# Adding the mirrored rows by accumulating DMAs instead of by VectorE, in a Fourier-mixing and leaky-ReLU kernel

## The chip, the cores and the metric

The kernel runs on one core of one Trainium2 chip. The metric is the device time of one execution in microseconds (us), the median of three runs. The profile is that of one execution, taken by the hardware profiler; its engines are PE (TensorE matmul), PEld (TensorE weight load), DVE (VectorE), ACT (ScalarE), POOL (GpSimd) and SP (SyncE, which here only issues DMAs). A name such as L287 is a line of the kernel before.

## The reference

```python
batch, seq, dim = (8, 3008, 256)          # x: float32
n_tokens, d_model, d_ff = (24064, 256, 2048)

def _attn_ref(x):
    X = np.fft.fft(x, axis=1)
    X = np.fft.fft(X, axis=2)
    return X.real.astype(np.float32)

def _moe_ref(x, w_in, w_out):
    h = x @ w_in
    g = np.maximum(0.01 * h, h)
    return (g @ w_out).astype(np.float32)

# x -> _attn_ref -> reshape to (B*S, D) -> _moe_ref
```

The real part of a two-dimensional Fourier transform of each batch is taken, and every row of it goes through an up projection, a leaky ReLU and a down projection.

## The kernel before

The cosine and sine transforms along the sequence use symmetries: row s and row S-s of x, and the half-turn rows around S/2, are added or subtracted before any matmul, so that a batch needs only a small part of the products. The host lays x out so that a row and its mirror lie at the same place of two planes: index 0 of the third axis of the tile is the row, index 1 its mirror.

```python
def x_tile():
    return xp.tile([LOADED, 2, 2, NT, D], F32, tag="x", bufs=1, name="xt")   # LOADED=128, NT=8, D=256

def load_x(b):
    t = x_tile()
    for h in range(2):
        for odd in range(2):
            load_rows(t, b, h, odd)
    return t

def load_rows(t, b, h, odd):                 # L280: 1024 KB each, four for a batch
    nc.sync.dma_start(t[:, h, :, odd * NI[0] : NI[0] + odd * NI[1]], x[b, h, odd])

def add_mirrors(t, h, rows):                 # L287
    a, z = t[:, h, 0, rows], t[:, h, 1, rows]
    nc.vector.tensor_tensor(a, a, z, op=ALU.add)

def fold_columns(t, h, part, rows):          # L294, L296
    a, z = t[:, h, 0, rows], t[:, h, 1, rows]
    if part == 0:
        nc.vector.tensor_tensor(z[:, :, 0:P], a[:, :, 0:P], a[:, :, P:D], op=ALU.add)
    else:
        nc.vector.tensor_tensor(z[:, :, P + 1 : D], a[:, :, 1:P], a[:, :, P + 1 : D], op=ALU.subtract)

def fold_halves(t, part, c, rows, to=None):  # L303: reads both z planes, writes t[:, i, 0]
    ...

def fold_x(b, at):                           # at = 0 .. 7
    t, rows = xs[b], slice(0, NT)
    h, i = divmod(at, 2)
    if h < 2 and i == 0:
        add_mirrors(t, h, rows)
    elif h < 2:
        for part in range(2):
            fold_columns(t, h, part, rows)
    else:
        fold_halves(t, i, 3 - h, rows)
    if at == 7:
        zs[b] = xs.pop(b)
```

The work is cut into 16 units (8 batches, each with the odd and the even frequencies), 3 blocks of about 251 columns in a unit and 8 steps `f` in a block: 384 steps. A step raises a block with two of the hidden layer's sixteen 128-row groups (`up`) and lowers the one of three steps earlier (`down`). The first two blocks use a plain form; the others use seven products instead of eight, for which GpSimd makes four sums `s1` to `s4`.

```python
def up(j, f):            # raised: 4 matmuls into two banks (L734), then activate:
    ...
    nc.vector.scalar_tensor_tensor(cos[:, hs], ...)          # L743, two of them
    nc.vector.tensor_tensor(g[:, 0], cos, sin bank, add)     # L747 (shortened)
    nc.vector.tensor_tensor(g[:, 1], cos, sin bank, subtract)# L748 (shortened)
    nc.scalar.activation(g, g, ACT.Lrelu)                    # L749
    nc.gpsimd.tensor_tensor(s1 ... s4)                       # L756 to L759

def down(j, f):
    if f == 0:
        banks = [sum_ps() for _ in range(4)]     # all four banks of the tag "sum"
    ...                                          # 7 matmuls, L801, in the order 0 1 5 6 4 2 3
    if f < NH - 1:
        return
    nc.scalar.copy(q1, p1)                       # L810
    for to, x, y in ((c11, q1, p2), (u2, q1, p6), (u3, u2, p7), (v, u2, p5),
                     (c22, u3, p5), (c12, v, p3), (c21, u3, p4)):
        nc.vector.tensor_tensor(to, x, y, op=ALU.add)        # L812
    put(o, n, first)

lag = 3
folds = {(0, 1): (0,), (0, 3): (1,), (0, 4): (2,), (0, 5): (3,), (0, 6): (4, 5), (0, 7): (6,), (1, 0): (7,)}

def step(at):
    j, f = steps[at]
    up(j, f)
    n, part = divmod(j, 3)
    b, c = units[n]
    if 0 < n < len(units) - 1:
        ...
        if n % 2 == 1 and (part, f) in folds:
            for i in folds[part, f]:
                fold_x(b + 1, i)
        if part > 0 and f == 3:
            fold_rows(units[n + 1], part - 1)    # ScalarE turns L323, L324; VectorE L326, L327 and others
        if part > 0 and f == 5:
            dft(units[n + 1], part - 1)          # matmuls from xt, L572
    if n % 2 == 0 and part == 2 and f == 6 and b + 1 < B:
        xs[b + 1] = load_x(b + 1)
    if at - lag >= done:
        down(*steps[at - lag])
```

The table `folds` says at which step the source asks for a part of the fold. In the main loop the tile framework orders each engine's instructions when the kernel is built, by its own estimate of when they are ready, and the engines run that fixed order on the chip: the fold of a batch comes some steps earlier than the table asks. The first batch is loaded and folded by other code ahead of the loop, which the change leaves as it is.

`turn`, which `fold_rows` uses, lets ScalarE write two scaled copies into the scratch that was the plane of the mirrored rows:

```python
nc.scalar.activation(tmp[0], y, ACT.Copy, scale=sin)   # L323
nc.scalar.activation(tmp[1], y, ACT.Copy, scale=cos)   # L324
```

Of the kernel before, what the change touches and what calls it, by code (L numbers as in the profile page):

```python
# [60 lines left out]
ALU = mybir.AluOpType  # L61
# [3 lines left out]
P = 128  # L65
H, Q = S // 2, S // 4

NI = [4, 4]
# [170 lines left out]
def tile_fnet_leaky_relu(  # L239
# [12 lines left out]
    nc = tc.nc  # L252
# [13 lines left out]
    def x_tile():  # L266
        return xp.tile([LOADED, 2, 2, NT, D], F32, tag="x", bufs=1, name="xt")
# [2 lines left out]
        return ps.tile([P, 512], F32, tag="sum", bufs=4, name="sum_ps")  # L270

    def load_x(b):
        t = x_tile()
        for h in range(2):
            for odd in range(2):
                load_rows(t, b, h, odd)
        return t

    def load_rows(t, b, h, odd):
        nc.sync.dma_start(t[:, h, :, odd * NI[0] : NI[0] + odd * NI[1]], x[b, h, odd])  # L280
# [3 lines left out]
# [5 lines that stand above are left out]
    def fold_columns(t, h, part, rows):  # L289
# [8 lines that stand above are left out]
    def fold_halves(t, part, c, rows, to=None):  # L298

        i, cols = (c + part) % 2, slice(part * P, (part + 1) * P)  # L300
        z = t[:, :, 1, rows, cols]
        to = t[:, i, 0, rows, cols] if to is None else to[:, rows]
        nc.vector.tensor_tensor(to, z[:, 0], z[:, 1], op=(ALU.add, ALU.subtract)[i])  # L303

    def fold_x(b, at):

        t, rows = xs[b], slice(0, NT)
        h, i = divmod(at, 2)
        if h < 2 and i == 0:
            add_mirrors(t, h, rows)  # L310
        elif h < 2:
            for part in range(2):
                fold_columns(t, h, part, rows)
        else:
            fold_halves(t, i, 3 - h, rows)
        if at == 7:
            zs[b] = xs.pop(b)
# [501 lines left out]
    def step(at):  # L819
        if at < len(steps):  # L820
# [4 lines that stand above are left out]
            if n == 0 and f in (2, 5):  # L825
                dft(units[1], f // 5)
            if 0 < n < len(units) - 1:
                if part == 0 and f == 4:
                    spread(units[n + 1])
# [4 lines that stand above are left out]
                    fold_rows(units[n + 1], part - 1)  # L834
                if part > 0 and f == 5:
                    dft(units[n + 1], part - 1)
# [4 lines that stand above are left out]
# [10 lines left out]
    with tc.manual_schedule(engines={mybir.EngineType.DVE, mybir.EngineType.PE, mybir.EngineType.SP}):  # L851
        with tc.manual_schedule(engines={mybir.EngineType.Pool, mybir.EngineType.Activation}):
# [8 lines left out]
            t = x_tile()  # L861
# [67 lines left out]
            odd = [direct.odd_rows(P, *first) for direct in (cosine, sine)]  # L929
# [6 lines left out]
            odd = [direct.odd_rows(P, *others) for direct in (cosine, sine)]  # L936
# [105 lines left out]
```

## Time and profile before

The median is 1901.75 us, of three runs from 1901.07 to 1901.96. The profiled execution has a span of 1900.0 us and a granted TensorE clock of 0.999.

| what | busy us, share of the span | instructions |
|---|---|---|
| PE | 1894.0, 100% | 9124 |
| PEld | 1684.1, 89% | 9124 |
| DVE | 1286.1, 68% | 2565 |
| POOL | 1113.6, 59% | 1509 |
| ACT | 502.0, 26% | 681 |
| DMA, all queues | 78.13 MB, mean 41 GB/s | 33052 packets |
| of it the loads of x (L280) | 32 of 1024 KB, median 9.1 us from issue to landing | |

How to read it: the busy share of an engine is an average over all stages. An engine that is idle costs nothing as long as the one that sets the end does not wait for it. PE's matmuls are pipelined and their ends are modelled, so a single matmul has a mean of 374 ns here while the next starts about 210 ns after it. In the timeline each row is the start in us, the duration in us, the engine, the line and operation, the tiles written and read, the shape and how many were merged into the row; square brackets tell the idle time ahead of it and what ended that.

### The profile page before, as it was taken

The numbers are of one execution on the slowest core, as the hardware profiler recorded it, in microseconds if no ns is written. First come the engines' busy times: TensorE is split into PE (matmuls) and PEld (weight loads), VectorE is DVE, ScalarE is ACT, GpSimd is POOL, SyncE is SP. The second block draws the span as 40 slices with busy tenths as digits, with TensorE's granted clock in tenths as the row PEclk, the third lists the DMA queues.
The fourth block names the chain that finished last, engine by engine and source line by source line (L and its number), as shares of the span: only waits on it lengthen the run. The fifth ranks groups of instructions, "written<-read, shape, count | busy, mean of one in ns | idle before, by whom it ended". The sixth has DMA issues, their size and how long they took to land.

```text
span 1900.0 us, 25328 instructions
## 1 busy us (share of the span) xinstructions
PE 1894.0 (100%) x9124; PEld 1684.1 (89%) x9124; DVE 1286.1 (68%) x2565; ACT 502.0 (26%) x681; POOL 1113.6 (59%) x1509
## 2 busy tenths in 40 slices
PE   9999999999999999999999999999999999999999
PEld 7888888988889888898888988889888888888988
DVE  8879755696656965569555796558865688556554
ACT  3532222222222322223222232222322223222221
POOL 2137655576555765558555575557655566555554
PEclk9999999999999999999999999999999999999999
DMA  7212000020002000020000200002000030000000
GB/s 274 78 31 108 12 20 22 30 90 12 31 12 85 34 20 22 12 108 11 23 20 12 108 23 12 19 12 108 23 12 20 12 119 12 20 12 23 12 11 23
DMA packets 33052, 78.13 MB, mean 41 GB/s; under 512 B 5264, under 2 KB 18960, under 8 KB 32928
## 3 DMA queue, kind: packets, MB, share of 16 engines
q1 hardware_dynamic: 32352, 76.52, 11.0%
q8 instruction: 73, 1.20, 0.3%
q14 instruction: 51, 0.42, 0.1%
q10 hardware_dynamic: 576, 0.00, 0.0%
HBM read 51.79 MB, written 24.71 MB: 40 GB/s over the span
## 4 chain that ended last, share of the span: by engine, by line
PE 98%; DMA 1%; DVE 0%; SPq 0%; issue 0%; DVEq 0%
PE sum_ps L801 58%; PE cos_ps L734 17%; PE sin_ps L734 17%; PE sum_ps L781 3%; PE dft_ps L572 3%; PE wf_ps L516 1%; DMA direct<-in_direct_tab_dram 1%; DMA xt<-in_x_dram 0%; PE dft_ps L399 0%; PE sum_ps L707 0%; DVE e L812 0%; DVE xt L287 0%; SPq L280 0%; SPq L449 0%; DVE differences L303 0%; DVE xt L294 0%
## 5 line engine op out<-in xcount | busy, mean ns | idle before, releaser
L749 ACT ACTIVATE g<-g 128x1004 f32<-128x1004 f32 (+1 forms) x384 | 399.2, 1040 | 1110.5 <-DVE g L748 1044.1
L743 DVE SCALAR_TENSOR_TENSOR cos<-nb,wn,cos_ps 128x251 f32<-128x251 f32 (+1 forms) x768 | 330.2, 470 | 517.5 <-PE cos_ps L734 514.2
L756 POOL TENSOR_TENSOR s<-g 128x251 f32<-128x251 f32 (+1 forms) x368 | 275.3, 748 | 655.9 <-ACT g L749 655.9
L801 PE MATMUL sum_ps<-s,wt 128*128 128x251 f32 (+1 forms) x2208 | 528.5, 374 | 0.0
L801 PEld LDWEIGHTS sum_ps<-s,wt 128*128 128x128 f32 x2208 | 415.0, 188 | 55.1 <-POOL s L757 2.2
L734 PE MATMUL cos_ps<-mix,wf 128*128 128x251 f32 (+1 forms) x1536 | 388.1, 375 | 0.0
L734 PE MATMUL sin_ps<-mix,wf 128*128 128x251 f32 (+1 forms) x1536 | 387.6, 374 | 0.0
L801 PE MATMUL sum_ps<-g,wo 128*128 128x251 f32 (+1 forms) x1472 | 373.0, 375 | 0.0
L757 POOL TENSOR_TENSOR s<-s,g 128x251 f32<-128x251 f32 (+1 forms) x368 | 325.4, 884 | 0.0
L734 PEld LDWEIGHTS cos_ps<-mix,wf 128*128 128x128 f32 x1536 | 291.1, 190 | 34.8 <-issue 1.1
L734 PEld LDWEIGHTS sin_ps<-mix,wf 128*128 128x128 f32 x1536 | 290.4, 189 | 34.6
L801 PEld LDWEIGHTS sum_ps<-g,wo 128*128 128x128 f32 x1472 | 276.9, 190 | 31.9
L759 POOL TENSOR_TENSOR s<-g,s 128x251 f32<-128x251 f32 (+1 forms) x368 | 275.2, 748 | 28.9
L747 DVE TENSOR_TENSOR g<-cos,sin_ps 128x502 f32<-128x502 f32 (+1 forms) x384 | 259.3, 675 | 42.6 <-DVE cos L743 5.7
L748 DVE TENSOR_TENSOR g<-cos,sin_ps 128x502 f32<-128x502 f32 (+1 forms) x384 | 256.9, 669 | 0.0
L758 POOL TENSOR_TENSOR s<-g 128x251 f32<-128x251 f32 (+1 forms) x368 | 249.1, 677 | 0.0
L801 PE MATMUL sum_ps<-g,wt 128*128 128x251 f32 (+1 forms) x736 | 215.8, 375 | 0.0
L801 PE MATMUL sum_ps<-s,wo 128*128 128x251 f32 (+1 forms) x736 | 215.8, 375 | 0.0
L801 PEld LDWEIGHTS sum_ps<-s,wo 128*128 128x128 f32 x736 | 139.4, 189 | 16.3
L801 PEld LDWEIGHTS sum_ps<-g,wt 128*128 128x128 f32 x736 | 139.8, 190 | 15.8
L812 DVE TENSOR_TENSOR o<-e,sum_ps 128x251 f32<-128x251 f32 (+1 forms) x184 | 67.4, 408 | 8.7 <-ACT e L810 8.7
L572 PEld LDWEIGHTS dft_ps<-tab,xt 95*128 95x128 f32 x480 | 58.3, 192 | 1.4
(119 smaller groups left out, 849.6 us busy)
## 6 DMA issues: line engine op xcount, KB each, us to landing
xt<-in_x_dram SPq DMA_DIRECT2D x32, 1024.0 KB, 9.1
out_dram<-o SPq DMA_DIRECT2D x80, 251.0 KB, 2.4
raw<-in_w_in_dram SPq DMA_DIRECT2D x8, 512.0 KB, 4.6
raw<-in_w_out_dram SPq DMA_DIRECT2D x8, 512.0 KB, 5.4
out_dram<-o SPq DMA_DIRECT2D x16, 250.0 KB, 2.2
nb<-nyq_dram SPq DMA_DIRECT2D x8, 376.5 KB, 3.2
nb<-nyq_dram SPq DMA_DIRECT2D x7, 376.0 KB, 4.0
direct<-in_direct_tab_dram SPq DMA_DIRECT2D x4, 376.0 KB, 5.1
```

The source lines that it names most:

```text
L572: nc.tensor.matmul(o, lhsT=still, rhs=moving, start=(i == 0), stop=(i == 3), skip_group_check=True)
L734: nc.tensor.matmul(pt[blk][:, h * n : (h + 1) * n], lhsT=wf[:, blk, fs[h] * P : (fs[h] + 1) * P], rhs=mixed[b, c][blk][:, at : at + n], st ...
L743: nc.vector.scalar_tensor_tensor(cos[:, hs], in0=spreads[b, c][:, at : at + n], scalar=wn[:, fs[h] : fs[h] + 1], in1=pt[0][:, hs], op0=ALU ...
L747: nc.vector.tensor_tensor(g[:, 0], cos[:, 0 : 2 * n], pt[1][:, 0 : 2 * n], op=ALU.add)
L748: nc.vector.tensor_tensor(g[:, 1], cos[:, 0 : 2 * n], pt[1][:, 0 : 2 * n], op=ALU.subtract)
L749: nc.scalar.activation(g, g, ACT.Lrelu)
L756: nc.gpsimd.tensor_tensor(s1, a[1][0], a[1][1], op=ALU.add)
L757: nc.gpsimd.tensor_tensor(s2, s1, a[0][0], op=ALU.subtract)
L758: nc.gpsimd.tensor_tensor(s3, a[0][0], a[1][0], op=ALU.subtract)
L759: nc.gpsimd.tensor_tensor(s4, a[0][1], s2, op=ALU.subtract)
L801: nc.tensor.matmul(sums[j][p], lhsT=still[p], rhs=moving[p], start=(f == 0 and i % 2 == 0), stop=(f == NH - 1), skip_group_check=True)
L812: nc.vector.tensor_tensor(to, x, y, op=ALU.add)
```

## The change

For all batches but the first, the plane of mirrored rows is no longer loaded. SyncE loads the rows (four DMAs of half the size), and for each of them a DMA on GpSimd's queue reads the mirrored rows from memory and adds them onto the loaded rows in the tile. VectorE's `add_mirrors` falls away for these batches, and the two column folds of a half, which were asked for together, are asked for one at a time. A small memset on GpSimd fills the one column of the mirrored plane that the loads used to fill. The purpose is to take work from VectorE, whose adds also keep GpSimd from its own work while they run.

```diff
     def load_x(b):
+
         t = x_tile()
         for h in range(2):
             for odd in range(2):
-                load_rows(t, b, h, odd)
+                rows = slice(odd * NI[0], NI[0] + odd * NI[1])
+                nc.sync.dma_start(t[:, h, 0, rows], x[b, h, odd][:, 0])
+                nc.gpsimd.dma_start(t[:, h, 0, rows], x[b, h, odd][:, 1], accum_op=ALU.add)
+            nc.gpsimd.memset(t[:, h, 1, :, P : P + 1], 0.0)
         return t
@@
         t, rows = xs[b], slice(0, NT)
         h, i = divmod(at, 2)
-        if h < 2 and i == 0:
-            add_mirrors(t, h, rows)
-        elif h < 2:
-            for part in range(2):
-                fold_columns(t, h, part, rows)
+        if h < 2:
+            fold_columns(t, h, i, rows)
         else:
             fold_halves(t, i, 3 - h, rows)
```

## The prediction

> **What bounds the kernel now.** I read the page's busy shares first, then the chain that ended last, then the waits, and last the timeline around one load of x.
>
> ```profile
> PE 1894.0 (100%) x9124; PEld 1684.1 (89%) x9124; DVE 1286.1 (68%) x2565; ACT 502.0 (26%) x681; POOL 1113.6 (59%) x1509
> PE 98%; DMA 1%; DVE 0%; SPq 0%; issue 0%; DVEq 0%
> ```
>
> TensorE is busy all the time, and 98% of the chain that ended last is TensorE's own work. Since matmul ends are modelled I checked the starts in the trace: the 9124 matmuls begin 1894 us apart from first to last, and nearly all of that lies in intervals of 200 to 220 ns, the pace of a 251-column matmul. So TensorE does not wait for VectorE in any sum that could be won back: **the change can take away hardly anything; it can only leave TensorE alone or make it wait.** The question is how much slack the places have that the change touches. The waits, the rows of the tile xt (minimum, median and maximum ns), and VectorE's timeline around the load of the third batch:
>
> ```profile
> DVE xt L287 <- DMA xt<-in_x_dram: 14.1, 9, 2.0
> L287 DVE TENSOR_TENSOR xt<-xt x18: 1216/2279/2845, 10.2 to 1548.7; 128x2048 f32<-128x2048 f32 x14, 128x1024 f32<-128x1024 f32 x4
> L294 DVE TENSOR_TENSOR xt<-xt x18: 692/1210/1673, 11.5 to 1551.7; 128x1024 f32<-128x1024 f32 x14, 128x512 f32<-128x512 f32 x4
> L303 DVE TENSOR_TENSOR xt<-xt x32: 683/1217/1556, 16.4 to 1567.3; 128x1024 f32<-128x1024 f32 x30, 128x512 f32<-128x512 f32 x2
> ...
> 375.89 2.55 SPq L280 DMA_DIRECT2D xt<-in_x_dram  x4
> ...
> 381.29 0.67 DVE L748 TENSOR_TENSOR g<-cos,sin_ps 128x500 f32<-128x500 f32 x1
> 383.81 2.83 DVE L287 TENSOR_TENSOR xt<-xt 128x2048 f32<-128x2048 f32 x1 [1.85 <-DMA xt<-in_x_dram]
> 386.55 0.85 DVE L743 SCALAR_TENSOR_TENSOR cos<-nb,wn,cos_ps 128x250 f32<-128x250 f32 x2
> ...
> 402.41 0.67 DVE L748 TENSOR_TENSOR g<-cos,sin_ps 128x502 f32<-128x502 f32 x1
> 403.00 0.40 DVE L812 TENSOR_TENSOR o<-e,sum_ps 128x250 f32<-128x250 f32 x1
> ...
> 403.58 1.01 PE L801 MATMUL sum_ps<-g,wo 128*128 128x251 f32 x4
> 404.58 1.57 PE L801 MATMUL sum_ps<-s,wt 128*128 128x251 f32 x6
> ```
>
> The loads are issued at 375.89. VectorE reaches the add at 382.0 and already waits 1.85 us there for the data. From 383.8 to 403.0 it is full, with two adds, five folds and the activations of four steps. At 403.0 it begins the block's last sums (L812), and the first of them frees the bank into which TensorE starts the next block's sums at 403.58; 403.4 would have been its own pace. **VectorE thus comes out of the fold just in time**, with about nothing to spare. It is the same in all seven batches: step for step, the smallest margins between GpSimd's sums and the matmul that uses them (1.0 to 1.8 us, against a median of 8.4) are at just these two steps of each load.
>
> GpSimd around the same load:
>
> ```profile
> 379.56 0.72 POOL L759 TENSOR_TENSOR s<-g,s 128x250 f32<-128x250 f32 x1
> 383.19 0.63 POOL L756 TENSOR_TENSOR s<-g 128x250 f32<-128x250 f32 x1 [2.90 <-ACT g L749]
> 383.77 0.71 POOL L758 TENSOR_TENSOR s<-g 128x250 f32<-128x250 f32 x1
> 384.44 2.77 POOL L757 TENSOR_TENSOR s<-s,g 128x250 f32<-128x250 f32 x1
> 387.29 0.63 POOL L759 TENSOR_TENSOR s<-g,s 128x250 f32<-128x250 f32 x1
> ```
>
> L757 normally takes 0.72 us; here it takes 2.77 because VectorE's add lies over it.
>
> **What the Trainium skill says.** "SBUF — State Buffer", section "SBUF: two separate sides", calls the port pair of VectorE and GpSimd an exclusive lock, also for a VectorE operation with two SBUF inputs beside a GpSimd operation that reads SBUF. The trace agrees (0.72 against 2.77 us), so dropping the adds does give GpSimd time. "DMA: Bandwidth & Descriptors", section "SWDGE vs HWDGE vs iDMA", says that accumulation is possible only for DMAs issued from GpSimd, whose descriptors are written by its cores; its "Anatomy of one DMA — SWDGE (gpsimd) path" gives about 2.0 us plus bytes / 436 GB/s, and its specifications about 1 us to the first byte. No DMA of this kind is in the trace before; the loads from SyncE agree in form (below).
>
> **The change part by part.**
>
> Removed: 14 adds of 2048 elements at a median of 2.28 us, 32 us of VectorE, all beside TensorE's work; worth nothing by itself. The wait for the loads (14.1 us in nine waits) is moved, not removed.
>
> Added: 14 memsets of 128x8 and 28 accumulating DMAs on GpSimd. I looked at the order in which the changed kernel's engines are built to run. TensorE's and SyncE's orders are unchanged. On GpSimd the sums of the step before the load's, then three accumulating DMAs, then three of the next step's four sums, then the fourth DMA, then the fourth sum. On VectorE the first column fold stands where the first add stood, after the g of one step and ahead of the next step's cos, and it waits for the two accumulating DMAs of its half. All eight folds now lie in four steps, each ahead of a cos or a pair of g. On ScalarE six of the turns (L323) have moved **ahead of the copy q1** (L810), on which the block's last sums depend; before, they came after it. A turn writes into the mirrored plane, which the last fold of halves still reads, so they wait for the eighth fold.
>
> When does the data come? In another load of the trace the four landed 5.4, 8.0, 10.6 and 13.1 us after the first issue: 2.55 us per 1024 KB and 2.9 us fixed. Halved loads, by the same numbers: 4.2, 5.4, 6.7 and 8.0 us. GpSimd is done with its sums at 380.3, which is 4.4 us after the issue, so it starts the first accumulating DMA at about 4.6, with the load just landed. I take 1 us for writing its descriptors, 2.9 us fixed and 1.3 us for the data if it runs like a load, or 2.55 if reading both the mirrored rows and the tile costs twice: landing at 9.8 to 11.0. The second follows behind it on the same engines: 11.0 to 13.6. I choose 12.2 us, that is 388.1 in this stretch, where the add used to start at 383.8.
>
> From then VectorE needs, to the end of the eighth fold: eight folds of 1.2 (9.6), four cos pairs of 0.8 (3.2), three pairs of g of 1.2 (3.6), and about 0.8 for GpSimd's lock: 17.2 us. Then six turns in ScalarE (L323 and L324 run six in 1.84 us), the copy of 0.37, the first sum of 0.40 and some 0.2 of hand-overs: 2.9 us more, so 388.1 + 20.1 = 408.2 instead of 403.4. **TensorE would wait 4.8 us at the block's edge.** Its other needs are met by then: psum banks for the second step after a g would wait only if the data came after about 387.9, by tenths, and this lies inside the same 4.8 us. After the edge VectorE has two folds less to do than before, so I expect no further wait. Sum: 7 batches x 4.8 = 34 us, and 1901.75 + 34 = 1936.
>
> **The rivals.** (a) All hidden: the accumulation lands at 383 or the sums keep up, and nothing is left: 1900 to 1904. For it: the DMA queues are nearly empty (41 GB/s on average) and from its data to the block's sums VectorE needs 17.2 us where it now takes 19.2 (383.8 to 403.0). Against it: VectorE waits already for the direct load, and a chain of two transfers can't land sooner than one; the data would have to be there by about 383.3. (b) GpSimd becomes the bound: the wait for a load and the descriptors stand in its queue ahead of the sums of the next step. At 8.2 us for the three DMAs the sums end around 386 to 388, and TensorE uses them at 394.3: no wait, unless a DMA holds GpSimd for more than 2 us each; that would also make the data late, and give 1960 or more. (c) Accumulation is slow, say 6 us for each 512 KB: then the second lands after 17 us, the wait is 9.5 us a batch, and the time about 1970.
>
> **Range and chances.** Each us by which the data come sooner or later is 7 us of the time. Between 9 and 16.5 us from issue to the second landing lie 1.6 and 9.1 us of wait, 1913 and 1966; with some room for (a) I take 1907 to 1966. The 2% mark is at 1939.8, that is 5.4 us a batch, close above my middle. Faster by 2% is out of reach, since TensorE's own work fills 1894 us.
>
> **What would show it.** The wait of VectorE at the first column fold for GpSimd's DMAs: 4 to 7 us, seven times, in place of 14.1 us in total. GpSimd's DMA rows of about 1 us, landing 5 to 8 us after issue. Waits of TensorE's L801 for VectorE's last sums (o, line +1), about 5 us, seven times, right after six ScalarE turns that wait for the eighth fold. TensorE's busy time should stay near 1894 us while the span grows past it. Wrong would be: no wait at these edges, waits on GpSimd's sums instead, or a stall spread over all steps.

## The result and the profile after

The changed kernel takes 1955.35 us (median of four runs, 1954.01 to 1956.05) against 1901.6 us before (median of four runs): a ratio of 1.0282 (95% interval 1.0266 to 1.0297), or 53.75 us more. This lies in the predicted range from 1907 to 1966, but 19 us above its middle, 1936: the added time was to be 34 us.

The page of the changed kernel, busy shares and the chain that ended last by engine:

```profile
PE 1909.5 (98%) x9124; PEld 1692.8 (87%) x9124; DVE 1245.5 (64%) x2551; ACT 501.9 (26%) x681; POOL 1091.9 (56%) x1551
PE 87%; DMA 6%; DVE 3%; issue 2%; POOL 1%; SPq 0%; DVEq 0%; POOLq 0%
```

VectorE and GpSimd are less busy, as meant, and the time is longer: TensorE's part of the chain fell from 98% to 87%, and DMA, VectorE and GpSimd now have 10% of it. The waits tell where (who waited for whom, total us, times, longest):

```profile
DVE xt L298 <- DMA xt<-in_x_dram: 65.1, 13, 9.6
PE sum_ps L802 <- DVE o L813: 23.7, 7, 3.4
POOL xt L279 <- DMA xt<-in_x_dram: 14.8, 14, 2.5
PE sin_ps L735 <- DVE g L749: 12.3, 13, 1.5
```

VectorE stands 65.1 us at the column folds (L298) for GpSimd's DMAs, seven times at the first fold and six times at the third, where it stood 14.1 us for the loads. TensorE waits seven times at the block's edge for VectorE's last sums, and besides at the second step after a late pair of g. One batch in full, from the timelines of SyncE, GpSimd, VectorE and TensorE (start, duration):

```profile
862.10 1.77 SPq L278 DMA_DIRECT2D xt<-in_x_dram  x4
...
866.37 0.86 POOL L279 DMA_DIRECT2D xt<-in_x_dram  x1
867.74 0.86 POOL L279 DMA_DIRECT2D xt<-in_x_dram  x1 [0.50 <-DMA xt<-in_x_dram]
869.95 0.86 POOL L279 DMA_DIRECT2D xt<-in_x_dram  x1 [1.35 <-DMA xt<-in_x_dram]
...
872.43 1.19 POOL L279 DMA_DIRECT2D xt<-in_x_dram  x1
...
875.93 1.23 DVE L298 TENSOR_TENSOR xt<-xt 128x1024 f32<-128x1024 f32 x1 [7.83 <-DMA xt<-in_x_dram]
...
881.37 1.23 DVE L298 TENSOR_TENSOR xt<-xt 128x1024 f32<-128x1024 f32 x1 [1.14 <-DMA xt<-in_x_dram]
...
894.25 0.67 DVE L749 TENSOR_TENSOR g<-cos,sin_ps 128x502 f32<-128x502 f32 x1
894.84 0.40 DVE L813 TENSOR_TENSOR o<-e,sum_ps 128x250 f32<-128x250 f32 x1
...
895.30 2.04 PE L802 MATMUL sum_ps<-g,wo 128*128 128x251 f32 x4 [3.42 <-DVE o L813]
```

The loads go out at 862.10. GpSimd issues its DMAs from 866.37 to 872.43, waiting in between for the second and third load. VectorE could have begun the first fold at 868.1 and begins it at 875.93, then waits once more, for the second half. It reaches the block's sums at 894.84, with no gap after g, and TensorE has stood 3.42 us when it starts again at 895.30.

One thing more is in this batch. Stretches of the timeline by engine, with the granted TensorE clock (PEclk):

```profile
core 0: us, PE busy (x) PEld busy (x) DVE busy (x) ACT busy (x) POOL busy (x), PEclk, DMA share, GB/s
862.00:876.00 14.00, 14.00 (x68) 12.58 (x68) 5.24 (x12) 2.41 (x4) 9.16 (x14) 1.00 0.90 243
896.00:900.00 4.00, 4.00 (x11) 3.24 (x10) 4.00 (x12) 0.80 (x3) 2.69 (x4) 0.50 0.34 130
```

At this wait TensorE's clock falls to half in six of the seven batches: five times for 3.41 us, beginning 0.9 to 1.5 us after TensorE has started again, and in the batch shown for 6.83 us, from 893.91 on, which is 1.4 us before TensorE starts. 11 matmuls lie in the 4 us of the second row and nine of them start there, where 19 would at the usual pace.

The account, from the intervals between matmul starts in the seven stretches after a load: intervals over 0.6 us, less the usual 0.21, come to 24.9 us at the block's edges (L802) and 16.4 us in the up matmuls (L735); intervals between 0.23 and 0.6 us lose 14.2 us, where the same stretches lost 2.0 before. That is 53.5 of the 53.75 us (24.9 + 16.4 + 12.2). Most of the 12.2 is the clock: TensorE works for 22.5 us at half clock, which loses half of that, 11.3 us.

### The profile page after: what moved, and what is told of

It is laid out like the page before. It is cut to its first block, busy times and chain, and to the rows that moved or that the text cites. A ratio compares the mean times of both kernels' runs of the same rounds, so it can differ in the third digit from the quotient of the medians.

```text
span 1953.4 us, 25420 instructions
## 1 busy us (share of the span) xinstructions
PE 1909.5 (98%) x9124; PEld 1692.8 (87%) x9124; DVE 1245.5 (64%) x2551; ACT 501.9 (26%) x681; POOL 1091.9 (56%) x1551
## 4 chain that ended last, share of the span: by engine, by line
PE 87%; DMA 6%; DVE 3%; issue 2%; POOL 1%; SPq 0%; DVEq 0%; POOLq 0%
PE sum_ps L802 50%; PE sin_ps L735 15%; PE cos_ps L735 15%; DMA xt<-in_x_dram 5%; PE sum_ps L782 3%; PE dft_ps L573 3%; DVE cos L744 1%; DVE g L748 1%; DVE xt L307 1%; DVE g L749 1%; PE wf_ps L517 1%; POOL xt L279 1%; DMA direct<-in_direct_tab_dram 0%; PE dft_ps L400 0%; POOL s L759 0%
## 5 line engine op out<-in xcount | busy, mean ns | idle before, releaser
L802 PE MATMUL sum_ps<-s,wt 128*128 128x251 f32 (+1 forms) x2208 | 534.8, 378 | 0.0
L802 PEld LDWEIGHTS sum_ps<-s,wt 128*128 128x128 f32 x2208 | 419.6, 190 | 54.7 <-issue 1.6
L735 PE MATMUL sin_ps<-mix,wf 128*128 128x251 f32 (+1 forms) x1536 | 388.8, 375 | 12.3 <-DVE g L749 12.3
L802 PE MATMUL sum_ps<-g,wo 128*128 128x251 f32 (+1 forms) x1472 | 374.7, 377 | 23.7 <-DVE o L813 23.7
L735 PE MATMUL cos_ps<-mix,wf 128*128 128x251 f32 (+1 forms) x1536 | 388.5, 375 | 1.6 <-DVE cos L744 1.6
L735 PEld LDWEIGHTS sin_ps<-mix,wf 128*128 128x128 f32 x1536 | 289.6, 189 | 51.0 <-issue 9.2
L802 PEld LDWEIGHTS sum_ps<-g,wo 128*128 128x128 f32 x1472 | 277.5, 190 | 57.5 <-DVE o L813 26.5
L735 PEld LDWEIGHTS cos_ps<-mix,wf 128*128 128x128 f32 x1536 | 291.8, 190 | 37.1 <-DVE cos L744 2.4
L758 POOL TENSOR_TENSOR s<-s,g 128x251 f32<-128x251 f32 (+1 forms) x368 | 289.2, 786 | 0.0
L802 PE MATMUL sum_ps<-s,wo 128*128 128x251 f32 (+1 forms) x736 | 218.5, 379 | 0.0
L802 PE MATMUL sum_ps<-g,wt 128*128 128x251 f32 (+1 forms) x736 | 217.4, 377 | 0.0
L802 PEld LDWEIGHTS sum_ps<-s,wo 128*128 128x128 f32 x736 | 141.4, 192 | 16.9
L802 PEld LDWEIGHTS sum_ps<-g,wt 128*128 128x128 f32 x736 | 141.5, 192 | 16.3
L298 DVE TENSOR_TENSOR xt<-xt 128x1024 f32<-128x1024 f32 (+1 forms) x18 | 21.0, 1165 | 65.3 <-DMA xt<-in_x_dram 65.1
```

Of the source, the lines that this page charges most:

```text
L735: nc.tensor.matmul(pt[blk][:, h * n : (h + 1) * n], lhsT=wf[:, blk, fs[h] * P : (fs[h] + 1) * P], rhs=mixed[b, c][blk][:, at : at + n], st ...
L758: nc.gpsimd.tensor_tensor(s2, s1, a[0][0], op=ALU.subtract)
L802: nc.tensor.matmul(sums[j][p], lhsT=still[p], rhs=moving[p], start=(f == 0 and i % 2 == 0), stop=(f == NH - 1), skip_group_check=True)
```

## The experiments

The theory: two transfers one after the other bring the data later than VectorE's fixed order wants them, and VectorE, which has little slack up to the block's edge, passes the delay to TensorE. Rivals: the new order itself (folds crowded into four steps, turns ahead of the copy q1); GpSimd's queue, whose DMA issues and waits hold up the sums s1 to s4; the DMA traffic.

**The same order, without the accumulating DMAs.** The folds and the cos and g beside them are pinned to the places they have in the changed kernel; all instructions of VectorE, ScalarE and TensorE stand in the changed kernel's order. The mirrored rows are left out of the sums. The edit, shortened:

```diff
-                nc.gpsimd.dma_start(t[:, h, 0, rows], x[b, h, odd][:, 1], accum_op=ALU.add)
+    # activate(), at the four steps where the changed kernel has its folds:
+    fold_x(b1, at1); cos; fold_x(b1, at1 + 1); g    # each by tc.keep_in_program_order
```

> The changed kernel with the instructions of VectorE, ScalarE and TensorE pinned to the very order of the changed kernel, but without the accumulating DMAs: the mirrored rows are left out of the sums. Late-data theory (VectorE stands at the first fold because two transfers follow one another): the data are the direct loads alone, landed before VectorE arrives some 6 us after the first issue, so no wait and 1899 to 1904 us. Rival, the order is to blame (folds crowded into four steps, turns ahead of the copy of the block's sums): about 1940 to 1955 us, with the same waits of TensorE at the block's edge.

Measured: 1900.33 us, ratio 0.9994 (0.9985 to 1.0002). In the main loop VectorE waits for a load once, in the first of the seven batches:

```profile
DVE xt L297 <- DMA xt<-in_x_dram: 2.5, 1, 2.5
```

TensorE has no interval over 0.6 us in the seven stretches, and the clock stays full. The order is not to blame.

**Plain copies instead of accumulation,** in the same order on every engine. The mirrored rows overwrite the rows, so the sum is left out.

```diff
-                nc.gpsimd.dma_start(t[:, h, 0, rows], x[b, h, odd][:, 1], accum_op=ALU.add)
+                nc.gpsimd.dma_start(t[:, h, 0, rows], x[b, h, odd][:, 1])
```

> The changed kernel in the same order on every engine, with GpSimd's DMAs as plain copies (the mirrored rows overwrite the rows; the sum is left out). If reading the tile for the addition is what makes these DMAs slow: landing 5 to 6.5 us after issue instead of 7 to 9.6, the first fold starts about 3 us sooner, TensorE's wait is that much shorter in each of seven batches, and 1922 to 1936 us. If the addition costs the DMA nothing (the queue or the two hops are all): about 1955 us as the changed kernel.

Measured: 1918.21 us, ratio 1.009 (1.0076 to 1.0103). GpSimd's DMAs, from the DMA view of both kernels (the changed one first; KB each, median us from issue to landing), and then the waits of VectorE and TensorE with the copies:

```profile
xt<-in_x_dram POOLq DMA_DIRECT2D x28, 512.0 KB, 8.4
```

```profile
xt<-in_x_dram POOLq DMA_DIRECT2D x28, 512.0 KB, 5.3
```

```profile
DVE xt L298 <- DMA xt<-in_x_dram: 38.4, 7, 7.3
PE sum_ps L802 <- DVE o L813: 12.4, 7, 3.3
```

The same bytes land 3.1 us sooner when they are not added. The two DMAs of the first half have landed 11.1 us after the first load's issue instead of 13.9 (medians over the batches), and VectorE waits 38.4 us instead of 65.1. TensorE's intervals over 0.6 us cost 13.5 us, all at the edge, instead of 41.3 (24.9 + 16.4), and the clock is halved after one wait instead of six, which loses 1.7 us instead of 11.3; together that is the 37.1 us that the time gains, within 0.3. Of the 53.75 us the addition in the DMA thus costs 37, a part of the clock's loss included, and what is left with plain copies, the second hop and GpSimd's queue, about 17.

**The folds later, in program order.** Each fold is pinned behind what the source has before it.

```diff
-            fold_columns(t, h, i, rows)
+            tc.keep_in_program_order(fold_columns(t, h, i, rows))
-            fold_halves(t, i, 3 - h, rows)
+            tc.keep_in_program_order(fold_halves(t, i, 3 - h, rows))
```

> The changed kernel with all its DMAs; each fold is pinned behind what the source has ahead of it on VectorE, so the first fold comes about two and a half steps (some 12 us) later and the eight are spread over eight steps. Late-data theory: the second accumulating DMA lands about 15.4 us after the first load's issue and VectorE now comes to the first fold at about 20, so no wait: 1897 to 1904 us. Rival, GpSimd's queue (its DMA issues and its waits for the loads hold up the sums s1 to s4): the DMAs stand in the same place, so 1935 us or more. Rival, DMA traffic itself slows the chip: the same, 1935 or more.

Measured: 1912.11 us, ratio 1.0056 (1.0042 to 1.007). A miss by 8 us, though not by the rivals' way: GpSimd's DMAs stand where they stood, VectorE's wait for them in the loop is gone, and none of the waits at the fold is left. The last fold now ends some 56 us after the load, and the next unit's `fold_rows`, which need the folds, keep VectorE busy up to a later block's edge, some 66 us after the load:

```profile
PE sum_ps L802 <- DVE o L813: 7.8, 7, 1.1
```

Each of the seven intervals there is 1.48 us instead of 0.21, together 8.9 of the 10.5 us above the kernel before. **The same pins on the kernel before** are the control.

> Control: the kernel before (VectorE adds the mirrored rows, one load) with its folds pinned the same way. If TensorE's pace is all there is to win, 1897 to 1902 us, and within 3 us of the changed kernel with pinned folds; if taking the adds from VectorE is worth something once the data come in time, it is slower than that one by more than 3 us.

Measured: 1918.36 us, ratio 1.0089 (1.0075 to 1.0103), against a forecast of at most 1902: a miss for the same reason. The seven intervals at that later edge are 2.1 to 2.3 us here, 4.6 us more in all, and after one of them the clock is halved for 3.41 us, another 1.7. With the folds in this bad place the adds cost 6 us (1918.36 less 1912.11): taking work off VectorE was worth something there, where VectorE is late. The next experiment tries a place where it is not.

**The crowded folds one and two steps later.** All DMAs, two folds a step as in the changed kernel, pinned as in the first experiment, only moved. The edit, shortened:

```diff
-    (first, 7), (first + 1, 0), (first + 1, 1), (first + 1, 2)         # the changed kernel's places
+    (first + 1, 0), (first + 1, 1), (first + 1, 2), (first + 1, 3)     # one step later
+    (first + 1, 1), (first + 1, 2), (first + 1, 3), (first + 1, 4)     # two steps later
```

> The changed kernel with all its DMAs and the folds as crowded as in it (two a step), pinned one step later: VectorE comes to the first fold about 10.7 us after the first load's issue instead of 6. Late-data theory: the two DMAs of the first half land at 13.8 in most batches, so a wait of about 3 us is left at the first fold; three pairs of folds then stand ahead of the block's sums instead of four, and TensorE's wait at the edge falls from some 6.4 us with the slowed clock after it to 0.3 to 1.5: 1902 to 1912 us. Rival, crowding of the folds: as before the pinning, above 1940 us. Without a TensorE wait over 2 us no halved clock is expected after it.

> The same, pinned two steps later: VectorE comes to the first fold at about 15.3 us and to the third at about 20, with landings at 13.8 and 19.2. Late-data theory: no wait for the DMAs in most batches, 1899 to 1902 us, below or level with the kernel before, since TensorE's own pace (1900.3 us with the mirrored rows left out) is the floor. If taking the adds off VectorE is worth anything it shows here: by that floor it can be no more than about 1.2 us.

Two steps later: 1901.07 us, ratio 0.9998 (0.9989 to 1.0006), as the theory has it. The adds taken off VectorE are worth nothing there that the interval could tell. One step later: 1930.61 us, ratio 1.0152 (1.0138 to 1.0166), a miss by 19 us. VectorE's waits for GpSimd's DMAs, one step later and then two:

```profile
DVE xt L298 <- DMA xt<-in_x_dram: 40.7, 14, 7.2
```

```profile
DVE xt L298 <- DMA xt<-in_x_dram: 3.0, 3, 2.6
```

The forecast had reckoned with 3 us in a batch, at the first half alone; it is 5.8, in two waits. The fourth DMA lands 19.7 to 22.8 us after the first load's issue, so the second half holds VectorE up again, TensorE's waits at the edge were 1.6 to 2.8 us in six batches and 4.1 in the first, and the clock was halved after five of the seven. With two steps one interval of 0.72 us is all that is left of TensorE's waits in the seven stretches, with the same DMAs at the same places in GpSimd's and SyncE's orders and the same traffic: both rivals fall.

**TensorE kept busy during its wait.** In the changed kernel the last up matmul ahead of the long wait is repeated eight times, into the same bank with the same result.

```diff
+        if j % 6 == 3 and f == 3 and j < len(blocks) - 3:
+            for _ in range(8):
+                tc.keep_in_program_order(nc.tensor.matmul(pt[1][:, n : 2 * n], ...same operands..., start=True, stop=True))
```

> The changed kernel with eight repeats of the last up matmul (same operands, same bank, 16 instructions or about 3.4 us at full pace) put into TensorE's order just ahead of its long wait at the block's edge, once in each of seven batches; VectorE's order is the same up to the block's sums. If idleness of TensorE is what halves its clock for 3.4 us afterwards, the repeats fill the wait, the clock stays at full speed and six times about 1.7 us are saved: 1943 to 1948 us. If the halved clock has another cause (the restart as such, the DMAs), it stays: about 1955 us. If the wait at the edge is shorter than it looks, the repeats cost time themselves: up to 1979 us.

Measured: 1942.42 us, ratio 1.0214 (1.0197 to 1.0231). VectorE waits about as long as in the changed kernel (63.4 us against 65.1), and TensorE, in the same batch as above, runs on through the wait:

```profile
887.12 3.55 PE L739 MATMUL sin_ps<-mix,wf 128*128 128x251 f32 x16
890.69 1.12 PE L806 MATMUL sum_ps<-g,wo 128*128 128x251 f32 x4
891.72 1.57 PE L806 MATMUL sum_ps<-s,wt 128*128 128x251 f32 x6
```

The eight repeats, 16 records since each float32 matmul stands there as two, fill the wait, the six matmuls after it take 1.57 us instead of 2.72, and the clock is full to the end of the kernel's work. 112 more records of matmuls (9236 against 9124) make the kernel 12.9 us faster. The half clock had cost 11.3 us; the up matmuls also wait somewhat less in this run, 13.4 us instead of 16.4. With the same DMAs and the wait filled no half clock is left: **it was TensorE's own idleness that halved its clock.** That the clock fell 1.4 us ahead of the restart in the batch shown speaks against the restart as the cause, too.

## Why the prediction was right, and where its terms were off

- **What bounds the kernel: right.** TensorE's pace was the floor and nothing could be won. With the mirrored rows left out it is 1900.33 us, and with the fold moved two steps 1901.07.
- **The place of the loss: right in the main.** VectorE waits at the first fold, seven times, and TensorE at the edge for the last sums, seven times. But the edge takes only 3.6 us a batch (24.9 / 7). Another 2.3 us (16.4 / 7) are lost before it, where up matmuls wait for psum banks that a late g frees; the prediction had tenths there.
- **Landing at 12.2 us after the loads' issue: too early.** The first accumulating DMA takes 7.0 us from issue in most batches, where I had 5.2 to 6.5. The second of the half lands at 13.7 to 13.9 in five batches and at 15.3 and 15.7 in two, past the end of my span (13.6): with the addition it mostly lands 2.5 us behind the first, with plain copies 1.3. The row of an issue lasts 0.87 us, near the 1 chosen. VectorE's wait at the first fold was to be 6.1 us and is 8.4 (58.5 / 7). By the fixed time and the rate that the prediction quotes, 512 KB would take 3.2 us (an estimate); on GpSimd's queue the plain copies took 5.3 and the accumulating DMAs 8.4.
- **The fourth DMA: left out.** It waits in GpSimd's queue behind the third, which waits for its load, and behind three sums, is issued 10.3 us after the loads (12.3 in the first batch) and lands at 18.8 to 20.7. VectorE stops a second time in six batches, 1.14 us in the batch shown; with these stops it waits 9.3 us a batch (65.1 / 7).
- **The turns ahead of q1: no cost.** I had them wait for the eighth fold and put 2.9 us behind it. The batch shown has, on ScalarE, VectorE (the eighth fold) and ScalarE:

```profile
891.45 1.86 ACT L324 ACTIVATE xt<-xt,angle 95x128 f32<-95x128 f32 x6
892.10 1.64 DVE L307 TENSOR_TENSOR xt<-xt 128x1024 f32<-128x1024 f32 x1
893.84 1.57 ACT L325 ACTIVATE xt<-xt,angle 95x128 f32<-95x128 f32 x5 [0.28 <-DVE xt L307]
```

The six turns (L324) start before the eighth fold: only the second copies (L325) wait for it. The sums follow straight on VectorE's g, and TensorE starts 1.56 us after the eighth fold in every batch. From the first fold to the edge the prediction had 20.1 us; it is 18.2 to 18.7 without the second stop. That excess of 1.4 to 1.9 us a batch hid part of the other two terms.
- **The clock: not foreseen.** The Trainium skill has it: "TensorE: Matmul & The Clock Gate", section "What's actually happening", tells of a clock at half rate after an idle window of about 3.4 us, in free-running windows of 3413 ns. The trace agrees on the length: 3413 ns at a granted clock of 0.5, or twice that (6827 ns in the batch shown). It does not agree on the idle time that is needed: one step late, intervals of 2.7 to 3.0 us between starts were enough, four times of four. The half clock cost 11.3 us here; the experiment that removed it gained 12.9, with somewhat shorter waits.
- **The sum.** 4.8 us a batch were forecast; 5.9 of waiting (41.3 / 7) and 1.7 of slowed matmuls (12.2 / 7) came. From the two kernels of one order, VectorE's wait less TensorE's is the slack there was: (65.1 - 41.3) / 7 = 3.4 us with accumulation, and (38.4 - 13.5) / 7 = 3.6 with plain copies. My slack was 1.3 (6.1 less 4.8). A wait one third too short and a slack almost two thirds too small partly cancelled. So it is partly luck that 34 us came as near to the 41 of waiting, and the clock's share lies in the range without having been thought of.
- **Three readings that were off.** The margins of 1.0 to 1.8 us (median 8.4) run to the first matmul of the step, which does not use GpSimd's sums; to the first that does they are 1.9 to 2.6 (9.2). After the edge VectorE has three folds less to do, not two: five of the eight stood ahead of it before. And rival (a) compared 17.2 us, up to the eighth fold, with 19.2, up to the sums; with the last pair of g the first is 18.4. None of the three moves the forecast.
- **The rivals.** (c), slow accumulation, was the nearest: not 6 us for each 512 KB in sequence, but about 2.5 us for each one behind the first, which took 7. Of (b), no matmul in the loop waits for GpSimd's sums.

## What to carry to other kernels

Taking work off an engine that is not the bound gave nothing here, and if its data then come by a longer way, an order fixed at build time turns that delay into a wait of the engine that is the bound: ask where the first reader of the new transfer stands and how much slack it has, not how busy the queues are. The cure is to move the reader, by just enough: two steps here gave back all of the 54 us, one step not quite half, and moving it as far as the source asks gave back 43 and ran into the next narrow place. No version tried beats the kernel before by more than the intervals allow, since TensorE's pace is reached.

## What the runs showed that I had not expected

- An accumulating DMA of 512 KB on GpSimd's queue took 8.4 us from issue to landing, a plain copy of the same bytes on the same queue 5.3. The row of an issue on GpSimd lasts mostly 0.86 us for the one (1.2 for the fourth of a batch) and 0.55 for the other. GpSimd is not held longer by it: its next sum begins 0.56 us after the start of the third issue with accumulation and 0.55 with plain copies, but then takes 0.96 us instead of 0.64.
- A single wait of TensorE cost more than its length. Starts 2.7 to 3.8 us apart brought half a clock in 11 of 12 cases (six of seven in the changed kernel, all four of that length one step late, one with the copies), ten times for 3.41 us and once for 6.83; an interval of 4.3 us brought 6.83, while intervals of 1.5 to 2.3 us brought it once in 25. What decides between such cases was not tested. The loss, 1.7 us for 3.41 us at half clock, could be avoided by matmuls that compute nothing new.
- One thing stays open: in the kernel that is one step late the fourth DMA lands later (20.5 us in the median) than in the changed kernel (19.4). The load of another tile (nb) is issued 9.3 us after the first load there, and 15.9 us in the changed kernel, so it may share the DMA engines with it. In the other runs with accumulation the two go together: with nb at 9.3 us the fourth lands at 20.8 (folds in program order and two steps late), with nb at about 16 at 19.2 (TensorE kept busy). No run isolates this.
